# Reordering the head and one change-over of a fused attention, dense-MLP and expert-MLP kernel

## The chip, the cores and the metric

The kernel runs on one core of a Trainium2 chip. The metric is the device time of one execution in microseconds; several executions are given by their median. The engines are PE (TensorE), DVE (VectorE), ACT (ScalarE), POOL (GpSimd) and SP, whose queue issues most DMAs. Each engine runs its own instructions in the order in which the program lists them, and waits on semaphores for the others.

## What is computed

```python
# attention: batch 4, 8 heads, 576 positions, head size 64
scores = q @ k.T / sqrt(64)
cum    = cumsum(max(s, 0))
scores = where(causal, -1e9, scores + minimum(-(cum_i - cum_j), 0))
attn   = softmax(scores)
x      = attn @ v                     # 2304 tokens x 512
# dense MLP, inner size 2048
x      = elu(x @ w_in) @ w_out
# eight experts, inner size 1024, the best one for each token
logits = x @ w_gate + modality_bias[modality_id]
out    = gate * (relu(x @ w1[e]) @ w2[e])
```

Products are made from fp32r operands split into a high and a low part (`qh`, `ql`, `kh`, `kl`, `gh`, `gl`), three matmuls for one product.

## The kernel before

`attention` (L43) works through 16 pairs of heads. For one pair, q and k are loaded as 96 partitions of six positions (`loads`, L103), turned by PE into PSUM and split by ACT (`qh`, `kh`) and DVE (`ql`, `kl`) (`qk`, L162); five blocks of scores S0 to S4 are made (`score`, L197); DVE adds the masked bias and takes row maxima (L236), ACT exponentiates (L243), PE turns the probabilities back (P0 to P4, L279 and L295), and V0 and V1 multiply them with v (`av`, L302). The masks of one pair (`b`, and the diagonal block inside `bias`) are written by POOL from the pair's bias (L136). PSUM has three buffers of two banks for all of this (`ps_t`) and two single banks (`l1_r`, called `l` in the trace).

The order of PE's work in one pair is a list of names written by hand: `ORDER0` for the first pair, `ORDER1` for the second, `ORDER` for the others, `LAST` at the end. "lq" in a list issues loads: q and k of the pair two ahead, then v of this one; "ld" issues the biases of the pair two ahead. SP's queue issues DMAs in that order, and a DMA that waits for a semaphore holds up those behind it.

**The head** (L58 to L68 and L434 to L463). s is loaded on 32 partitions, one for each batch and head; `sums_s` makes the running sums on DVE and stores them to DRAM (`cumd`). From there every later pair's bias is loaded broadcast to 128 partitions (`biases`, L121). The first pair doesn't take that way: `spread` (L443) multiplies, for each of its two heads, a 32-row selector `sel` with the 32 rows of sums, and ACT copies the result to `bias`, in two pieces of 256 and 320 columns. `warm(n)` issues n small matmuls that nothing reads. PE's order in the head is: 40 warm matmuls, q turned, 4 warm, the first spread, k turned, the second spread, 5 warm, the scores S0, S1, S2.

**The change-over** (L1267 to L1277). The dense MLP works on five chunks of tokens in steps f; a step is a first product (`l1`, 12 matmuls of 512 columns, L663 to L665, then ACT and DVE make `gh` and `gl`), and a second product (`l2`, 12 matmuls into four `acc` banks, L998 to L1000). A queue keeps second products two steps behind. The first two first products (`first_step`, L695, "F0" and "F1" in `LAST`) run inside the attention's end, just ahead of V0 and V1 of the last pair. After the attention the loop over `steps` begins with (0, 2); as two steps wait in the queue it first does the second product of step 0, and then the first product of step 2. The `acc` and `tr` rings take the six banks that the attention's `ps_t` has left, `tr` first.

Of the kernel before, what the change touches and what calls it, by code (L numbers as in the profile page):

```python
# [7 lines left out]
F32 = mybir.dt.float32  # L8
# [34 lines left out]
def attention(tc, cst, q, k, v, s, xT, rsd, score_r, extra, first):  # L43
    nc = tc.nc
    B, H, S, D = q.shape
    NP = B * H // 2
    R = B * H
    with ExitStack() as ctx:
# [6 lines left out]
        ident = cst["ident"]  # L55
# [1 line left out]

        cumd = dr.tile([R, S], F32, name="cumd")  # L58
        scr = p1.tile([128, 2, 5, S], F32, tag="pt", name="scr")
        cum, s8, z = (scr[0:R, 0, i] for i in range(3))  # L60
        nc.sync.dma_start(s8, s.rearrange("b h s -> (b h) s"))
        nc.vector.memset(z, 0.0)

        def sums_s():
            nc.vector.tensor_scalar(out=s8, in0=s8, scalar1=0.0, scalar2=8.0, op0=ALU.max, op1=ALU.mult)
            nc.vector.tensor_tensor_scan(out=cum, data0=s8, data1=z, initial=0.0, op0=ALU.add, op1=ALU.add)
            nc.vector.tensor_scalar(out=s8, in0=cum, scalar1=cum[:, S // 2:S // 2 + 1], scalar2=None, op0=ALU.subtract)
            nc.sync.dma_start(cumd, s8)  # L68

        one = st.tile([128, 1], F32, name="one")  # L70
        nc.vector.memset(one, 1.0)
# [31 lines left out]
        def loads(p):  # L103
            b, hp = divmod(p, H // 2)
            d = T[p] = {}

            def qks(which="qk"):
                for n in which:
                    x = {"q": q, "k": k}[n]
                    d[n + "n"] = t = p2.tile([TP, TB, 2, D], F32, tag=n + "n", name=n + "n")  # L110
                    for h in range(2):
                        (nc.scalar if p == 0 and h else nc.sync).dma_start(t[:, :, h], x[b, 2 * hp + h].rearrange("(p t) d -> p t d", t=TB))

            def vs():
                d["vn"] = vn = p2.tile([128, 5, 2, D], F32, tag="vn", name="vn")
                m, r = rows(v, b, hp)
                for h in range(2):
                    nc.sync.dma_start(vn[:, 0:4, h], m[:, :, h])
                nc.sync.dma_start(vn[0:64, 4], r)

            def biases():  # L121
                d["bias"] = bias = p2.tile([128, 2, S], F32, tag="bias", name="bias")
                r0 = b * H + 2 * hp
                nc.sync.dma_start(bias.rearrange("p h s -> p (h s)"),
                                  cumd[r0:r0 + 2].rearrange("h s -> (h s)").unsqueeze(0).to_broadcast([128, 2 * S]))
            d["vs"] = vs
            return qks, biases
# [219 lines left out]
        def unit(p, o):  # L347

            if o[0] == "F":
                return first(int(o[1]))  # L350
            if o[0] == "X":
                x = extra.get((p, int(o[1])))
                return (0, [], x) if x else None
            if o[-1] == "'":
                p, o = p - 1, o[:-1]
            if o[0] == "S":
                return score(p, int(o[1])) if p < NP else None
            if o in OUT:
                return OUT[o](p - 1) if 1 <= p <= NP else None
            if o in ("lq", "ld"):  # L360
                if o == "ld":
                    return 0, extra.get((p, "ld"), []) + ([later.pop(p)] if p in later else []), []
                fs = []
                if p + 2 < NP:
                    qks, later[p] = loads(p + 2)
                    fs = [qks]
                return 0, fs + [T[p]["vs"]], []
            return PREP[o](p + 1) if p + 1 < NP else None
# [62 lines left out]
            for ch in chains:  # L431
                add(now[0] + HOP, d, ch)

        l0, l1 = loads(0), loads(1)  # L434

        sel = scr[0:R, 1, 0, 0:256].rearrange("p (h n) -> p h n", h=2)
        for h in range(2):
            nc.vector.tensor_copy(sel[:, h], ident[0:R, h:h + 1].to_broadcast([R, 128]))
        for f in (l0[0], lambda: l1[0]("k"), sums_s, lambda: l1[0]("q"), l1[1]):
            f()  # L440
        bias = T[0]["bias"] = p2.tile([128, 2, S], F32, tag="bias", name="bias")

        def spread(u, n):  # L443

            def pe():
                x["t"] = t = ps_t.tile([128, 2, 512], F32, tag="t", name="tb")
                for j in range(2):
                    nc.tensor.matmul(t[:, j, 0:n], sel[:, j], s8[:, u:u + n], start=True, stop=True)

            def out():  # L450
                nc.scalar.activation(out=bias[:, :, u:u + n], in_=x["t"][:, :, 0:n], func=AF.Copy)
            x = {}
            return (n / 300, 0, 0), [pe], [[("a", 0.11 + n / 560, out)]]

        warm(WARM)
        u = PREP["q"](0)
        q5 = [u[2][0].pop()]
        for i, x in enumerate((u, spread(0, 256), PREP["k"](0), spread(256, S - 256))):
            issue(x, T[0])
            if i == 0:  # L460
                warm(FILL1)
        run(now[0] + 2.5)
        warm(FILL0)  # L463
        m0 = masks(0)
# [54 lines left out]
def moe(tc, ctx, c, xT, rsd, wi, wo, mid, wg, mb, w1, w2, out, n_pre=3, dbg={}):  # L519
# [144 lines left out]
            nc.tensor.matmul(h, a, xl[:, k], start=False, stop=False)  # L664
            nc.tensor.matmul(h, b, xh[:, k], start=False, stop=(k == KD - 1))  # L665

    def l1(i, f, cu=((), (), ()), tail=()):
        n = chunks[i][1]
        xh, xl = X[i]
        w = W[f]  # L670
        h = l1_r(n)
        l1_mm(h, w, xh, xl)

        for u in tail:
            u()
        for u in cu[0]:
            u()
        er, ghr, glr = (e_r, gh_r, gl_r) if n > 256 else (e_h, gh_h, gl_h)
        e = er(n)
        nc.scalar.activation(out=e, in_=h, func=AF.Relu, scale=-1.0)  # L680
        nc.scalar.activation(out=e, in_=e, func=AF.Exp, scale=-1.0)  # L681
        for u in cu[1]:
            u()
        nc.vector.scalar_tensor_tensor(out=e, in0=e, scalar=-1.0, in1=h, op0=ALU.add, op1=ALU.max)  # L684
        for u in cu[2]:
            u()
        gh = ghr(n)
        gl = glr(n)
        nc.scalar.activation(out=gh, in_=e, func=AF.Copy)  # L689
        nc.vector.tensor_tensor(out=gl, in0=e, in1=gh.bitcast(F32), op=ALU.subtract)  # L690
        G[i, f] = gh, gl
# [47 lines left out]
    rpi_r = Ring(m, 2, 4, I32, "rpi")  # L739
    sr = {}  # L740
    ix_r = Ring(m, 3, 4, I32, "ix")
    tr_r, acc_r = (Ring(ps, n, 512, F32, k) for n, k in ((2, "tr"), (4, "acc")))

    x2d = dbg.get("x2d") or dr.tile([NT + 1, DM], F32, name="x2d")
    wgd = dr.tile([E, DM], F32, name="wgd")
# [519 lines left out]

    ctx.enter_context(tc.manual_schedule(engines=None))
    for i, f in steps:  # L1267
        while len(queue) >= (3 if i == NC - 1 and f > 1 else 2):
            second_product()
        for u in plan.pop((i, f - 0.5), []):  # L1270
            u()
        tail = []
        if i + 1 < NC and f == NF - 1:
            tail = [u[z][2] for u in xu for z in (2, 3)]
        if i == 0 and n_ma <= f + 3 < NF:
            conv_load(f + 3)
        l1(i, f, conv_units(f) if i == 0 else ((), (), ()), tail)  # L1277
        queue.append((i, f))
        if i + 1 < NC:
            if f == NF - 4:  # L1280
                xu = load_x(i + 1)
                for u in xu:
                    u[0][2]()
            if f == NF - 2:
                for u in xu:
                    u[1][2]()
        for u in plan.pop((i, f), []):
            u()
# [163 lines left out]
```

## Time and profile before

| | us |
|---|---|
| runs | 817.70, 817.62, 816.43 |
| median | 817.62 |
| the profiled execution | 818.49 |
| its span, first to last instruction | 816.7 |

| engine | busy us | share of the span |
|---|---|---|
| PE (matmul) | 802.4 | 98% |
| DVE | 560.8 | 69% |
| ACT | 448.6 | 55% |
| POOL | 164.0 | 20% |

Start times in the rows are microseconds from the start of the span. A row's second number is how long one instruction, or the run of `xN` equal ones, was busy; square brackets give the idle time of the engine just ahead of it and what ended it. In the chain of work that ended last, PE has 93% of the span. The mean granted TensorE clock is 0.995 of full speed.

### The profile page before, as it was taken

The numbers are of one execution on the slowest core, as the hardware profiler recorded it, in microseconds if no ns is written. First come the engines' busy times: TensorE is split into PE (matmuls) and PEld (weight loads), VectorE is DVE, ScalarE is ACT, GpSimd is POOL, SyncE is SP. The second block draws the span as 40 slices with busy tenths as digits, with TensorE's granted clock in tenths as the row PEclk, the third lists the DMA queues.
The fourth block names the chain that finished last, engine by engine and source line by source line (L and its number), as shares of the span: only waits on it lengthen the run. The fifth ranks groups of instructions, "written<-read, shape, count | busy, mean of one in ns | idle before, by whom it ended". The sixth has DMA issues, their size and how long they took to land.

```text
span 816.7 us, 14160 instructions
## 1 busy us (share of the span) xinstructions
PE 802.4 (98%) x5037; PEld 682.2 (84%) x5037; DVE 560.8 (69%) x1291; ACT 448.6 (55%) x917; POOL 164.0 (20%) x264
## 2 busy tenths in 40 slices
PE   8999999999999999999999999999999999999995
PEld 7787877877888888888888888899999999999995
DVE  7888888876998587356755575475777656565652
ACT  5898888863776433343334333445655555555542
POOL 5665645530000000200001000203012222212110
PEclk9999999999999999999999999999999999999998
DMA  8998998445644510022000200014737776666651
GB/s 195 241 219 214 222 221 185 137 145 178 201 155 129 190 51 1 1 93 63 1 1 12 92 1 1 1 53 150 222 120 261 256 255 219 231 217 214 222 183 39
DMA packets 123074, 114.14 MB, mean 140 GB/s; under 512 B 67752, under 2 KB 97704, under 8 KB 122866
## 3 DMA queue, kind: packets, MB, share of 16 engines
q1 hardware_dynamic: 118114, 102.87, 43.3%
q0 software_dynamic: 3696, 9.98, 3.4%
q8 instruction: 42, 0.69, 0.4%
q10 hardware_dynamic: 1184, 0.30, 0.2%
q14 instruction: 38, 0.31, 0.1%
HBM read 98.63 MB, written 14.75 MB: 139 GB/s over the span
## 4 chain that ended last, share of the span: by engine, by line
PE 93%; ACT 2%; DVE 2%; DMA 1%; issue 1%; POOL 1%; SPq 0%; POOLq 0%; ACTq 0%
PE acc L998 8%; PE acc L999 8%; PE acc L1000 8%; PE l L665 8%; PE l L664 8%; PE l L663 8%; PE av L315 5%; PE l L1070 4%; PE l L1069 4%; PE l L1068 4%; PE tp L279 4%; PE acc L1089 4%; PE acc L1090 4%; PE acc L1091 4%; PE l L220 3%; PE sc L229 1%
## 5 line engine op out<-in xcount | busy, mean ns | idle before, releaser
L680 ACT ACTIVATE e<-l 128x512 f32<-128x512 f32 (+1 forms) x78 | 43.1, 553 | 147.6 <-PE l L665 138.0
L684 DVE SCALAR_TENSOR_TENSOR e<-e,l 128x512 f32<-128x512 f32 (+1 forms) x78 | 49.3, 632 | 78.1 <-ACT e L681 76.6
L882 POOL DMA_INDIRECT lst<-tk,rpi x18 | 18.4, 1021 | 381.2 <-DVE tk L878 193.4
L243 ACT ACTIVATE pr<-pr,mx 128x128 f32<-128x128 f32 (+4 forms) x144 | 82.5, 575 | 4.9 <-DVE mx L236 3.3
L663 PE MATMUL l<-xsa,wb 128*128 128x512 f32 (+1 forms) x220 | 80.9, 368 | 0.0
L664 PE MATMUL l<-xsa,wb 128*128 128x512 f32 (+1 forms) x220 | 80.9, 368 | 0.0
L665 PE MATMUL l<-xsa,wb 128*128 128x512 f32 (+1 forms) x220 | 80.9, 368 | 0.0
L690 DVE TENSOR_TENSOR gl<-e,gh 128x512 fp32r<-128x512 f32 (+1 forms) x78 | 49.7, 637 | 43.5 <-PE acc L1000 23.0
L998 PE MATMUL acc<-wb,gh 128*128 128x512 f32 x198 | 77.6, 392 | 0.0
L999 PE MATMUL acc<-wb,gh 128*128 128x512 f32 x198 | 77.2, 390 | 0.0
L1000 PE MATMUL acc<-wb,gl 128*128 128x512 f32 x198 | 77.0, 389 | 0.0
L1074 DVE SCALAR_TENSOR_TENSOR gl<-l,gh 128x512 fp32r<-128x512 f32 x36 | 24.9, 690 | 72.3 <-ACT gh L1073 72.3
L689 ACT ACTIVATE gh<-e 128x512 fp32r<-128x512 f32 (+1 forms) x78 | 45.8, 587 | 51.8 <-DVE e L684 51.8
L1073 ACT ACTIVATE gh<-l 128x512 fp32r<-128x512 f32 x36 | 21.5, 597 | 92.7 <-PE l L1070 92.7
L1057 DVE TENSOR_TENSOR wb<-rawa,wb 128x512 fp32r<-128x512 f32 x110 | 68.7, 684 | 3.2 <-ACT e L1321 2.8
L136 POOL TENSOR_SCALAR_AFFINE_SELECT b<-bias 64x576 f32<-64x576 f32 (+3 forms) x80 | 50.6, 651 | 59.9 <-DVE mx L236 52.3
L1056 ACT ACTIVATE wb<-rawa 128x512 fp32r<-128x512 f32 x110 | 60.6, 627 | 0.0
L315 PE MATMUL av<-pt,vn 128*64 128x288 f32 (+4 forms) x512 | 50.2, 342 | 0.0
L1070 PE MATMUL l<-xsa,wb 128*128 128x256 f32 x168 | 47.5, 283 | 0.0
L1069 PE MATMUL l<-xsa,wb 128*128 128x256 f32 x168 | 47.5, 283 | 0.0
L664 PEld LDWEIGHTS l<-xsa,wb 128*128 128x128 f32 x220 | 41.4, 188 | 7.3
L663 PEld LDWEIGHTS l<-xsa,wb 128*128 128x128 f32 x220 | 41.4, 188 | 7.3
(265 smaller groups left out, 2210.5 us busy)
## 6 DMA issues: line engine op xcount, KB each, us to landing
rawa<-in_moe_w_dram SPq DMA_DIRECT2D x80, 512.0 KB
bias<-cumd SPq DMA_DIRECT2D x15, 576.0 KB
rawa<-in_moe_w_in_dram SPq DMA_DIRECT2D x10, 512.0 KB
rawa<-in_moe_w_out_dram SPq DMA_DIRECT2D x10, 512.0 KB
xT<-xo SPq DMA_DIRECT2D x16, 288.0 KB
qn<-in_q_dram SPq DMA_DIRECT2D x31, 144.0 KB
kn<-in_k_dram SPq DMA_DIRECT2D x31, 144.0 KB
vn<-in_v_dram SPq DMA_DIRECT2D x32, 128.0 KB
```

Source lines behind the costliest of these rows:

```text
L243: nc.scalar.activation(out=e[:, 0:w], in_=e[:, 0:w], func=AF.Exp, scale=-1.0, bias=d["mx"][:, i:i + 1], accum_out=sums[p % 2][:, i:i + 1])
L315: nc.tensor.matmul(o[64 * h:64 * h + 64, z, a - 288 * z:e - 288 * z], vn[0:r, j, h], pt[0:r, h, j, a:e], start=(j == 0), stop=(j == js - 1))
L663: nc.tensor.matmul(h, a, xh[:, k], start=(k == 0), stop=False)
L664: nc.tensor.matmul(h, a, xl[:, k], start=False, stop=False)
L665: nc.tensor.matmul(h, b, xh[:, k], start=False, stop=(k == KD - 1))
L998: nc.tensor.matmul(o, gh[:, s], a, start=(f == 0), stop=False)
L999: nc.tensor.matmul(o, gh[:, s], b, start=False, stop=False)
L1000: nc.tensor.matmul(o, gl[:, s], a, start=False, stop=last)
L1056: nc.scalar.activation(out=w[:, x], in_=raw[:, x], func=AF.Copy)
L1057: nc.vector.tensor_tensor(out=w[:, y], in0=raw[:, x], in1=w[:, x].bitcast(F32), op=ALU.subtract)
L1069: nc.tensor.matmul(h[:, j], a, xs[1][:, k], start=False, stop=False)
L1070: nc.tensor.matmul(h[:, j], b, xs[0][:, k], start=False, stop=(k == KD - 1))
```

## The change

Five edits:

1. s is loaded twice, on partitions 0 to 31 and 32 to 63, and its running sums are made on 64 partitions. `sel` has head 0's selector on the first 32 and head 1's on the second, so the two matmuls of a spread read different rows of the array.
2. In the head, the first pair's k is turned directly behind q, and both spreads come after it.
3. The third pair's k is issued on SP's queue ahead of the second pair's biases (`l2[0]("k")`, then `l1[1]()`); in the first pair's "lq" only the third pair's q is left.
4. At the change-over the first product of step 2 comes ahead of the second product of step 0, which is then called from inside `l1` (`mid`), ahead of the writing of `gh`.
5. The `acc` ring takes its banks ahead of `tr`.

```diff
-        cum, s8, z = (scr[0:R, 0, i] for i in range(3))
-        nc.sync.dma_start(s8, s.rearrange("b h s -> (b h) s"))
+        cum, s8, z = (scr[0:2 * R, 0, i] for i in range(3))
+        nc.sync.dma_start(s8, s.rearrange("b h s -> (b h) s").unsqueeze(0).to_broadcast([2, R, S]))
...
-            nc.sync.dma_start(cumd, s8)
+            nc.sync.dma_start(cumd, s8[0:R])
...
-                    qks, later[p] = loads(p + 2)
+                    qks, later[p] = loads(p + 2) if p else (lambda: l2[0]("q"), l2[1])
...
-        l0, l1 = loads(0), loads(1)
-
-        sel = scr[0:R, 1, 0, 0:256].rearrange("p (h n) -> p h n", h=2)
+        l0, l1, l2 = (loads(p) for p in range(3))
+
+        sel = scr[0:2 * R, 1, 0, 0:128]
         for h in range(2):
-            nc.vector.tensor_copy(sel[:, h], ident[0:R, h:h + 1].to_broadcast([R, 128]))
-        for f in (l0[0], lambda: l1[0]("k"), sums_s, lambda: l1[0]("q"), l1[1]):
+            r = slice(R * h, R * h + R)
+            nc.vector.tensor_copy(sel[r], ident[r, R * h + h:R * h + h + 1].to_broadcast([R, 128]))
+        for f in (l0[0], lambda: l1[0]("k"), sums_s, lambda: l1[0]("q")):
             f()
...
-                    nc.tensor.matmul(t[:, j, 0:n], sel[:, j], s8[:, u:u + n], start=True, stop=True)
+                    nc.tensor.matmul(t[:, j, 0:n], sel[R * j:R * j + R], s8[R * j:R * j + R, u:u + n], start=True, stop=True)
...
-            return (n / 300, 0, 0), [pe], [[("a", 0.11 + n / 560, out)]]
+            return (n / 600, 0, 0), [pe], [[("a", 0.11 + n / 560, out)]]
...
-        for i, x in enumerate((u, spread(0, 256), PREP["k"](0), spread(256, S - 256))):
+        for i, x in enumerate((u, PREP["k"](0), spread(0, 256), spread(256, S - 256))):
             issue(x, T[0])
             if i == 0:
                 warm(FILL1)
+            if i == 1:
+                l2[0]("k")
+                l1[1]()
...
-    def l1(i, f, cu=((), (), ()), tail=()):
+    def l1(i, f, cu=((), (), ()), tail=(), mid=None):
...
         for u in cu[2]:
             u()
+        if mid:
+            mid()
         gh = ghr(n)
...
-    tr_r, acc_r = (Ring(ps, n, 512, F32, k) for n, k in ((2, "tr"), (4, "acc")))
+    acc_r, tr_r = (Ring(ps, n, 512, F32, k) for n, k in ((4, "acc"), (2, "tr")))
...
-        while len(queue) >= (3 if i == NC - 1 and f > 1 else 2):
+        begun = (i, f) != steps[0]
+        while begun and len(queue) >= (3 if i == NC - 1 and f > 1 else 2):
             second_product()
...
-        l1(i, f, conv_units(f) if i == 0 else ((), (), ()), tail)
+        l1(i, f, conv_units(f) if i == 0 else ((), (), ()), tail, None if begun else second_product)
```

How instructions stand on the engines, at the three places that the prediction speaks of. First ACT in the head, before; `qh` and `kh` are the split of the first pair's q and k, `bias<-tb` the copies of the two spreads, and the rows of L243 are the first exponentials:

```order
L180 ACTIVATE qh<-tq 128x576
L451 ACTIVATE bias<-tb 128x2x256
L180 ACTIVATE kh<-tk 128x576
L451 ACTIVATE bias<-tb 128x2x320
L243 ACTIVATE pr,sums_134<-pr,mx 128x128 x2
```

and in the changed kernel:

```order
L180 ACTIVATE qh<-tq 128x576
L180 ACTIVATE kh<-tk 128x576
L452 ACTIVATE bias<-tb 128x2x256
L452 ACTIVATE bias<-tb 128x2x320
L243 ACTIVATE pr,sums_134<-pr,mx 128x128 x2
```

`kh` has moved past the first copy of a spread. PE's order has moved in the same way: six turns of k, then the two spreads.

Second SP's queue in the head, before (`L112` are loads of q and k, the first `qn` x2 being the second pair's, `L124` is the second pair's bias, `L118` and `L119` the first pair's v):

```order
L68 DMA cumd<-scr 32x576
L112 DMA qn<-in_q_dram 96x6x64 x2
L124 DMA bias<-cumd 128x1152
L112 DMA qn<-in_q_dram 96x6x64 x2
L112 DMA kn<-in_k_dram 96x6x64 x2
L118 DMA vn<-in_v_dram 128x4x64 x2
L119 DMA vn<-in_v_dram 64x2x64
```

and in the changed kernel:

```order
L68 DMA cumd<-scr 32x576
L112 DMA qn<-in_q_dram 96x6x64 x2
L112 DMA kn<-in_k_dram 96x6x64 x2
L124 DMA bias<-cumd 128x1152
L112 DMA qn<-in_q_dram 96x6x64 x2
L118 DMA vn<-in_v_dram 128x4x64 x2
L119 DMA vn<-in_v_dram 64x2x64
```

The third pair's k has moved past the second pair's bias and past the third pair's q.

Third PE at the change-over, before; `av` is the last pair's output, `gh_99` and `gl_101` are the operands of step 0's second product, `wa_88` the weights of step 2:

```order
L319 MATMUL av<-ident,rs 9x128
L998 MATMUL acc_3264<-wa_86,gh_99 128x512
L999 MATMUL acc_3264<-wa_86,gh_99 128x512
L1000 MATMUL acc_3264<-wa_86,gl_101 128x512
...
L663 MATMUL l_104<-xsa_95,wa_88 128x512
L664 MATMUL l_104<-xsa_96,wa_88 128x512
L665 MATMUL l_104<-xsa_95,wa_88 128x512
```

and in the changed kernel:

```order
L319 MATMUL av<-ident,rs 9x128
L667 MATMUL l_104<-xsa_95,wa_88 128x512
L668 MATMUL l_104<-xsa_96,wa_88 128x512
L669 MATMUL l_104<-xsa_95,wa_88 128x512
...
L1004 MATMUL acc_3262<-wa_86,gh_99 128x512
L1005 MATMUL acc_3262<-wa_86,gh_99 128x512
L1006 MATMUL acc_3262<-wa_86,gl_101 128x512
```

Twelve matmuls into `l_104` have moved past twelve matmuls into the `acc` banks. Behind these 24 the order on PE is as before.

## Rows read from the trace of the kernel before

**Rows 1.** Waits of PE, 0 to 30 us: who for whom, total us, times, longest
```profile
PE tk L173 <- DMA kn<-in_k_dram: 1.6, 1, 1.6
PE tp L279 <- DVE rt L94: 0.2, 1, 0.2
```
**Rows 2.** Waits of PE, 190 us to the end
```profile
PE acc L1342 <- DVE gl L1331: 0.2, 1, 0.2
```
**Rows 3.** Windows at the change-over: length, busy PE, PEld, DVE, ACT, POOL, PEclk, DMA, GB/s
```profile
184.50:186.10 1.60, 0.00 (x0) 0.00 (x0) 0.91 (x4) 1.17 (x2) 0.00 (x0) 1.00 0.00 0
187.00:188.00 1.00, 1.00 (x4) 0.81 (x3) 0.96 (x2) 0.00 (x0) 0.00 (x0) 0.50 0.36 137
```
**Rows 4.** Timeline of PE and its weight loads at the change-over
```profile
184.15 0.28 PE L319 MATMUL av<-ident,rs 128*9 128x128 f32 x1
186.13 0.19 PEld L998 LDWEIGHTS acc<-wa,gh 128*128 128x128 f32 x1 [1.90 <-DVE rt L94]
190.58 0.40 PE L663 MATMUL l<-xsa,wa 128*128 128x512 f32 x1
```
**Rows 5.** Timeline of DVE at the change-over
```profile
181.29 0.68 DVE L713 SCALAR_TENSOR_TENSOR e<-e,l 128x512 f32<-128x512 f32 x1
185.81 0.27 DVE L94 COPY rt<-av 9x128 f32<-9x128 f32 x1
```
**Rows 6.** Timeline of ACT behind the change-over, first instruction of steps 2 and 3
```profile
193.54 0.60 ACT L680 ACTIVATE e<-l 128x512 f32<-128x512 f32 x1 [7.83 <-PE l L665]
198.98 0.60 ACT L680 ACTIVATE e<-l 128x512 f32<-128x512 f32 x1 [2.63 <-PE l L665]
```
**Rows 7.** Timeline of PE in the head
```profile
6.32 1.13 PE L448 MATMUL tb<-scr 32*128 32x256 f32 x4
7.37 0.71 PE L173 MATMUL tk<-ident,kn 96*128 96x96 f32 x6
...
9.89 0.28 PE L220 MATMUL sc<-kl,qh 64*128 64x256 f32 x2
...
10.37 0.28 PE L220 MATMUL sc<-kh,ql 64*128 64x256 f32 x2
...
16.94 0.69 PE L173 MATMUL tk<-ident,kn 96*128 96x96 f32 x6 [1.59 <-DMA kn<-in_k_dram]
17.46 1.04 PE L279 MATMUL tp<-ident,pr 128*128 128x128 f32 x8
```
**Rows 8.** Timeline of ACT in the head
```profile
7.48 0.60 ACT L451 ACTIVATE bias<-tb 128x512 f32<-128x512 f32 x1 [0.63 <-PE tb L448]
8.12 0.65 ACT L180 ACTIVATE kh<-tk 128x576 fp32r<-128x576 f32 x1
...
16.12 0.71 ACT L243 ACTIVATE pr<-pr,mx 128x512 f32<-128x512 f32 x1
```
**Rows 9.** Timeline of POOL in the head
```profile
8.15 0.98 POOL L136 TENSOR_SCALAR_AFFINE_SELECT b<-bias 128x256 f32<-128x256 f32 x2 [5.49 <-ACT bias L451]
...
10.33 2.19 POOL L136 TENSOR_SCALAR_AFFINE_SELECT b<-bias 64x576 f32<-64x576 f32 x3
```
**Rows 10.** Timeline of DVE in the head
```profile
10.82 0.29 DVE L236 CUSTOM_DVE_ANT_0 pr<-sc,b 128x128 f32<-128x128 f32 x1 [1.25 <-PE sc L220]
...
11.93 0.55 DVE L236 CUSTOM_DVE_ANT_0 pr<-l,b 128x384 f32<-128x384 f32 x1
...
18.41 0.76 DVE L184 TENSOR_TENSOR kl<-tk,kh 128x576 fp32r<-128x576 f32 x1
...
20.07 0.69 DVE L236 CUSTOM_DVE_ANT_0 pr<-l,bias 128x512 f32<-128x512 f32 x1
```
**Rows 11.** Windows in the head, columns as in rows 3
```profile
14.00:16.00 2.00, 1.35 (x12) 1.03 (x12) 2.00 (x7) 2.00 (x7) 1.94 (x3) 1.00 0.65 98
16.00:18.00 2.00, 1.06 (x11) 1.09 (x12) 2.00 (x4) 1.19 (x5) 0.73 (x3) 1.00 0.72 171
```
**Rows 12.** SP's queue in the head, the third pair's k
```profile
9.47 1.40 SPq L112 DMA_DIRECT2D kn<-in_k_dram  x2
```

## The prediction

> **What bounds the kernel now.** I read the page first: PE is busy for 98% of the span and has 93% of the chain that ended last. So an edit pays only where PE stands still or runs below full speed. The view of PE's waits says where that is. From 190 us to the end it names one wait, of 0.2 us [rows 2]: whatever PE gains before 190 us reaches the end undiminished. In the first 30 us it names the wait for the third pair's k, 1.6 us, and one of 0.2 us [rows 1].
>
> The change-over is the other place. PE's weight loader stands still for 1.90 us until DVE has copied `rt` out of the last `av` bank, because the first `acc` bank lies there [rows 4, 5]. The windows show what follows: the granted clock is 1.00 while PE stands still, and 0.50, the 1.2 GHz level, from 187 to 188 us [rows 3]. Twelve matmuls then take from 186.13 to 190.58 us, 4.45 us [rows 4]. A step of 24 matmuls at full clock takes 5.44 us, from 193.54 to 198.98 [rows 6], so twelve are worth 2.72.
>
> In the head, PE's own time is not the measure. From 16 to 18 us PE is busy for 1.06 us of 2, while DVE is busy for all of it, and DVE is full from 14 to 16 us too [rows 11]. PE waits there, but DVE is the engine that cannot go faster.
>
> **The change, part by part.**
>
> *The change-over.* The first product of step 2 needs a free `l_104`, which DVE's read of step 0 gives back at 181.29 + 0.68 = 181.97 us [rows 5]. Its weights and tokens were split during the attention. So it can follow L319, at 184.15 us, directly, and the 1.90 us are gone. It takes 2.72 us and ends near 187.0; the `rt` copy ends at 185.81 + 0.27 = 186.08 [rows 5], so the second product of step 0 finds its banks free and PE stands still nowhere. With no standstill I expect no fall of the clock: 4.45 - 2.72 = 1.73 us more. Together 1.90 + 1.73 = 3.63 us, say **3.6**. What the move delays: `gh` of step 2 now waits for the end of step 0's second product, near 189.7 us. It is wanted only by the second product of step 2, which comes 24 matmuls, 5.44 us, after that, and needs the ACT and the DVE pass of about 0.65 us each. That cover holds. The swap of the rings costs nothing, since its first user arrives 0.9 us after the `rt` copy.
>
> *k ahead of the spreads.* k's six turns take the place of the first spread at 6.32 us and end at 6.32 + 0.71 = 7.03 [rows 7]. Before, `kh` started 0.04 us after the turns ended (8.12 against 7.37 + 0.71) [rows 7, 8]; now it starts at 7.08 and ends at 7.73, 1.04 us sooner. So the scores S0 and S1, which end at 10.37 + 0.28 = 10.65 and for which DVE waits until 10.82 [rows 7, 10], end some 0.9 us sooner. But the first copy of a spread now stands behind `kh` on ACT.
>
> *Two spreads at once.* No row shows two 32-row matmuls side by side. The nearest are the scores, pairs of 64-row matmuls of 256 columns: from 9.89 to 10.37 us are four pairs, 0.12 us a pair [rows 7], while one matmul of 512 columns takes 5.44 / 24 = 0.227, so one of 256 about 0.11. A pair costs what one costs. I take the same for 32 rows: the first spread shrinks from 1.13 to about 0.57 us and ends at 7.60. At the other end it stays 1.13 and ends at 8.16.
>
> *What POOL makes of it.* The copy starts when `kh` is done, 7.75, takes 0.60 and ends at 8.35. POOL's first mask came 0.07 us after the copy's end (8.15 against 7.48 + 0.60) [rows 8, 9]; now it comes at 8.42, 0.27 later than before. Without overlap of the two matmuls it is 8.16 + 0.04 + 0.60 + 0.07 = 8.87, 0.72 later. POOL then has no pause until the three masks that start at 10.33 and take 2.19 us; the second of them, the one for S2, ends near 11.8, and DVE takes S2's maximum at 11.93 [rows 9, 10]. POOL was 0.1 us from being late. So the 0.9 us won at S0 and S1 are lost again at S2: DVE takes the early maxima, waits for POOL, and takes S2's near 12.1, 0.2 later than before.
>
> The first spread shows ACT waiting 0.63 us for PE ahead of the copy, and the copy 0.60 us long [rows 8]. The Trainium skill, "TensorEngine Tiling (Array Packing)", section PSUM Bottleneck, says that using parts of the array side by side speeds up the matmuls and not the copying out of PSUM, which can then be the limit. By that rule the overlap is worth little here, since `kh` and the copy set POOL's start; by the rows it still keeps 8.87 - 8.42 = 0.45 us from being lost. No run here shows it yet, and the sum below would be the same under both, as the copy is counted in full.
>
> *k of the third pair earlier.* PE waits 1.59 us for it, until 16.94, though SP issued it at 9.47 [rows 7, 12]: about 7.4 us from issue to use. It now goes out behind the second pair's q, once k of the first pair is turned, near 7.1 us, 2.4 us sooner; so it lands by about 14.5 and PE's wait of 1.59 us goes. What is late next: the turn of the last exponentials, which on ACT end at 16.12 + 0.71 = 16.83 [rows 8], so P3 can start there and not at 17.46 [rows 7]; and DVE, which is full until `kl` of the third pair at 18.41 [rows 10, 11]. `kl` hung on the late k, but by little: DVE, full until 18.00, was idle for at most 0.4 us ahead of it, of which I take half. The next maxima, at 20.07, wait for the scores behind P3, and DVE could have taken them about 0.1 us sooner. So the 1.6 us shrink to 0.3.
>
> *The same k, other side.* The second pair's bias now goes out behind k, near 8.5 us. It feeds POOL's masks of the second pair, whose last, the sixth, is wanted at 20.07 [rows 10]. At 2.19 / 3 = 0.73 us a mask [rows 9], six take 4.4 us: the bias may land as late as 15.7. With the 7.4 us of the slowest load that the rows show, it lands at 15.9. That is a cost of 0.2 at most, and I count none.
>
> *The doubled s* is one more 72 KB load, and the sums on 64 partitions are as long as on 32 (their length is the row's). They were done before 6.32 us, when the first spread read them [rows 7], and are wanted at 7.03 now. Nothing.
>
> *The head in sum.* 0.2 late at S2, of which DVE's next wait, for ACT's `kh` of the second pair, gives 0.1 back; 0.3 gained at k of the third pair: **0.2 gained**. Bounds: 0.9 gained, if POOL isn't late and all of S0's lead gets through; 0.5 lost, if the two matmuls don't overlap (0.72 at POOL, less 0.2).
>
> **The sum.** 3.6 + 0.2 = 3.8 us off. The profiled execution took 818.49 us, its span 816.7; that gives 814.7 for the like of it. It lies 0.87 above the median of the runs, 817.62, so against the median: **813.8 us**.
>
> **The rivals.**
>
> *The clock falls all the same.* The fall at 187 us could hang on something else than the standstill, as PE stood still for 1.59 us at 15 to 17 us and the clock stayed at 1.00 there [rows 7, 11]. Then only the 1.90 us go, and 1.73 stay: 1.9 + 0.2 = 2.1 off, 815.5 us. For it: that second standstill, nearly as long, without a fall. Against it: the only fall of the middle comes directly behind the longest standstill.
>
> *The head's lead gets through.* If POOL starts as early as before, S2 and all behind it move with S0: 0.9 instead of 0.2, 813.1 us. For it: PE, ACT and DVE all have the lead. Against it: POOL's 0.1 us of slack.
>
> *The change doesn't do what it says.* The first product of step 2 waits for something that the order of PE doesn't show, or the second product meets a wait as long behind it. Then the 3.6 us stay and only the head's 0.2 are left: 817.4 us. Against it: DVE is done with `l_104` 2.2 us before PE needs it.
>
> *Slower than before.* One mechanism: the second pair's bias, behind k in SP's queue. Each microsecond by which it lands after 15.7 us puts off the second pair's maxima, and PE behind them. It eats up 3.6 us where it lands after 19.3 us; at 21 us the kernel ends at 817.6 - 3.6 + 5.3 = 819.3 us. For it: loads of the head are slow, 7.4 us for k. Against it: it would need 10.8 us, half as long again as the slowest one seen.
>
> **How the numbers follow.** 0.2% is 1.6 us, about what a measurement of this kernel can tell from no change. Forecast 0.70, head's lead 0.12, clock 0.10, no effect at the change-over 0.05, late bias 0.03. The first three are faster by more than 1.6 us: 0.92. No effect is within 0.2%: 0.05. Slower: 0.03. The range takes in the head's lead at the low end (813.1, less 0.6 as the runs lie apart by 1.27) and the clock at the high end (815.5 and 0.2): 812.5 to 815.7.
>
> **What would show it.** At the change-over: the first product of step 2 directly behind L319 of the last pair, no wait named for `rt`, PEclk 1.00 from 184 to 191 us, and step 3's first ACT row 3.6 + 0.2 sooner than 198.98, near 195.2. In the head: `kh` near 7.1 us, the first mask near 8.4, S2's maximum at 12.0 to 12.2 with an idle time ended by POOL, no wait for the third pair's k, and the maximum of 20.07 near 19.8. The prediction is wrong if the clock falls at another place, if a load of weights that PE now reaches 3.8 us sooner isn't there, or if S2's maximum comes before 11.5 us.

## The result, and the profile after

The changed kernel takes **821.70 us** (median of 6 runs, 821.23 to 822.02) and the kernel before 817.02 us (median of 6) beside it. The ratio is **1.0055, with a 95% interval of 1.0042 to 1.0068**: slower by 4.7 us, where 813.8 us and a gain of 3.8 were forecast; it is outside the range of 812.5 to 815.7 too. The runs of the kernel before lie further apart than the 1.27 us of the table, 815.7 to 820.0 us over all that follows, so the comparisons below are ratios with intervals.

Span of the profiled execution: 820.2 us, against 816.7. Its waits of PE in the first 30 us, and those of DVE (who for whom, total us, times, longest), answer to [rows 1]:

```profile
PE tq L173 <- DMA qn<-in_q_dram: 4.5, 1, 4.5
PE tp L279 <- DVE pt L94: 1.3, 1, 1.3
...
DVE scr L65 <- DMA scr<-in_s_dram: 6.2, 1, 6.2
```

The wait for the third pair's k is gone, as forecast. A wait for the *first* pair's q stands in its place, which no line of the prediction speaks of, and the sums wait 6.2 us for s. The windows of the changed kernel (length, busy time of PE, PEld, DVE, ACT, POOL, granted clock, DMA share, GB/s) show what the transfers do meanwhile:

```profile
4.00:6.00 2.00, 1.57 (x15) 1.30 (x13) 0.00 (x0) 0.00 (x0) 0.00 (x0) 1.00 1.34 178
6.00:8.00 2.00, 0.00 (x0) 0.00 (x0) 0.00 (x0) 0.00 (x0) 0.00 (x0) 1.00 1.17 133
8.00:10.00 2.00, 0.00 (x0) 0.00 (x0) 1.10 (x2) 0.00 (x0) 0.00 (x0) 1.00 0.17 30
```

From 4 to 6 us, with the loads under way, the view gives a DMA share of 1.34. From 8 us it is 0.17, and 30 GB/s move, until 11 us: by 0.17 / 1.34 x 16 that is, as an estimate, the work of two engines of 16. DVE has the doubled s, issued first, at 8.87 us, where it was 2.73 before. The 312 packets from 8.5 to 11 us are all under 512 bytes, where a row of s has 2304: what still comes then was issued behind s, as q was, for which PE waits until 10.05 us. PE's turns of q before, and the start of its work in the changed kernel, with DVE's maximum behind it, from the timelines (start, duration, engine, line, operation, tiles; idle time ahead in brackets), answer to [rows 7, 10]:

```profile
5.36 0.80 PE L173 MATMUL tq<-ident,qn 96*128 96x96 f32 x6
```
```profile
10.05 1.20 PE L173 MATMUL tq<-ident,qn 96*128 96x96 f32 x6 [4.48 <-DMA qn<-in_q_dram]
...
11.46 1.17 PE L173 MATMUL tk<-ident,kn 96*128 96x96 f32 x6
12.56 2.29 PE L449 MATMUL tb<-scr 32*128 32x256 f32 x8
...
16.02 0.41 PE L220 MATMUL sc<-kh,ql 64*128 64x256 f32 x2
16.24 0.41 PE L220 MATMUL sc<-kh,qh 64*128 64x256 f32 x2
16.45 0.41 PE L220 MATMUL sc<-kl,qh 64*128 64x256 f32 x2
...
27.14 0.69 DVE L236 CUSTOM_DVE_ANT_0 pr<-l,bias 128x512 f32<-128x512 f32 x1
```

q's turns start at 10.05 us. k's six turns take 1.17 us and not 0.71, and the pairs of the scores follow each other by 0.21 us and not by 0.12 [rows 7]: TensorE runs at nearly half its pace, until 20.0 us. (The clock's column reads 1.00 there, but this trace has no clock record before 20.07 us; the last section shows what that means.) Both together are the loss: the maximum that stood at 20.07 [rows 10] stands at 27.14 us, 7.07 later, and the last pair's L319 starts 7.17 later than at 184.15 [rows 4].

The change-over did what was forecast. PE's timeline there, ACT's first instructions of steps 1 and 3, and two windows, for [rows 3, 4, 6]:

```profile
191.32 0.28 PE L319 MATMUL av<-ident,rs 128*9 128x128 f32 x1
191.36 0.47 PE L667 MATMUL l<-xsa,wa 128*128 128x512 f32 x1
...
189.69 0.58 ACT L713 ACTIVATE e<-l 128x512 f32<-128x512 f32 x1
...
202.54 0.60 ACT L684 ACTIVATE e<-l 128x512 f32<-128x512 f32 x1 [5.03 <-PE l L669]
...
191.00:193.00 2.00, 2.00 (x14) 1.62 (x13) 1.30 (x3) 1.17 (x2) 0.00 (x0) 1.00 0.00 0
193.00:195.00 2.00, 2.00 (x10) 1.65 (x10) 1.97 (x4) 0.60 (x1) 0.00 (x0) 1.00 0.43 160
```

The first product of step 2 (L667) follows L319 directly, the granted clock stays at 1.00, and PE names no wait for `rt`. From ACT's first instruction of step 1 to that of step 3 are 12.85 us. Before it was 16.44, from 182.54 to 198.98 [rows 6]:

```profile
182.54 0.58 ACT L707 ACTIVATE e<-l 128x512 f32<-128x512 f32 x1
```

So the change-over gives 3.59 us, the head takes 7.15 (189.69 against 182.54), and 3.56 of loss are left, which is the spans' difference of 3.5.

### The profile page after: what moved, and what is told of

It is laid out like the page before. It is cut to its first block, busy times and chain, and to the rows that moved or that the text cites. A ratio compares the mean times of both kernels' runs of the same rounds, so it can differ in the third digit from the quotient of the medians.

```text
span 820.2 us, 14161 instructions
## 1 busy us (share of the span) xinstructions
PE 803.4 (98%) x5037; PEld 683.7 (83%) x5037; DVE 561.2 (68%) x1291; ACT 449.4 (55%) x917; POOL 165.5 (20%) x264
## 4 chain that ended last, share of the span: by engine, by line
PE 95%; ACT 1%; DVE 1%; DMA 1%; issue 0%; POOL 0%; SPq 0%; POOLq 0%; DVEq 0%
PE acc L1004 8%; PE l L669 8%; PE l L668 8%; PE l L667 8%; PE acc L1005 8%; PE acc L1006 8%; PE av L315 5%; PE l L1076 4%; PE l L1075 4%; PE l L1074 4%; PE tp L279 4%; PE acc L1095 4%; PE acc L1096 4%; PE acc L1097 4%; PE l L220 3%; PE sc L229 1%
## 5 line engine op out<-in xcount | busy, mean ns | idle before, releaser
L243 ACT ACTIVATE pr<-pr,mx 128x128 f32<-128x128 f32 (+4 forms) x144 | 82.5, 575 | 5.8 <-DVE mx L236 4.3
L667 PE MATMUL l<-xsa,wb 128*128 128x512 f32 (+1 forms) x220 | 80.9, 368 | 0.0
L1076 PE MATMUL l<-xsa,wb 128*128 128x256 f32 x168 | 47.5, 283 | 0.0
L1075 PE MATMUL l<-xsa,wb 128*128 128x256 f32 x168 | 47.5, 283 | 0.0
L1074 PE MATMUL l<-xsa,wb 128*128 128x256 f32 x168 | 47.5, 283 | 0.0
L668 PEld LDWEIGHTS l<-xsa,wb 128*128 128x128 f32 x220 | 41.4, 188 | 7.3
```

The lines of the kernel that those rows point to most:

```text
L243: nc.scalar.activation(out=e[:, 0:w], in_=e[:, 0:w], func=AF.Exp, scale=-1.0, bias=d["mx"][:, i:i + 1], accum_out=sums[p % 2][:, i:i + 1])
L667: nc.tensor.matmul(h, a, xh[:, k], start=(k == 0), stop=False)
L1074: nc.tensor.matmul(h[:, j], a, xs[0][:, k], start=(k == 0), stop=False)
L1075: nc.tensor.matmul(h[:, j], a, xs[1][:, k], start=False, stop=False)
L1076: nc.tensor.matmul(h[:, j], b, xs[0][:, k], start=False, stop=(k == KD - 1))
```

## The experiments

Twelve kernels were timed, in 5 to 12 executions each. "q" is the start of q's turns, "last pair" the start of `kl` of the last pair (what the head is late by is read there), "steps 1 to 3" the change-over's stretch as above; these three are from each kernel's profiled execution, in us.

| kernel | us | before | ratio, 95% interval | q | last pair | steps 1 to 3 |
|---|---|---|---|---|---|---|
| before | | | | 5.36 | 153.91 | 16.44 |
| the change | 821.70 | 817.02 | 1.0055 (1.0042 to 1.0068) | 10.05 | 161.05 | 12.85 |
| e1 two loads | 814.97 | 817.92 | 0.9966 (0.9954 to 0.9979) | 6.18 | 156.51 | 12.87 |
| e2 doubled s alone | 825.32 | 817.92 | 1.0088 (1.0073 to 1.0102) | 9.74 | 163.34 | 16.43 |
| e2b copies inner | 818.13 | 818.02 | 1.0009 (0.9993 to 1.0024) | 6.44 | 154.93 | 16.43 |
| e3 change-over alone | 815.56 | 817.92 | 0.9968 (0.9956 to 0.9980) | 5.36 | 155.32 | 12.83 |
| e4 head, two loads | 818.20 | 817.92 | 0.9994 (0.9983 to 1.0005) | 6.40 | 156.32 | 14.81 |
| e5 q first | 816.91 | 818.02 | 0.9982 (0.9970 to 0.9994) | 4.79 | 156.94 | 12.89 |
| e6 more fillers | 814.82 | 818.02 | 0.9959 (0.9945 to 0.9972) | 6.49 | 155.36 | 12.88 |
| e7 q first, old head | 820.59 | 818.02 | 1.0032 (1.0019 to 1.0045) | 5.04 | 159.89 | 12.85 |
| e9 second subtraction | 814.20 | 817.86 | 0.9961 (0.9947 to 0.9974) | 5.73 | 156.30 | 12.89 |
| e10 with 45 fillers | 814.32 | 817.86 | 0.9959 (0.9944 to 0.9973) | 5.46 | 154.85 | 12.88 |
| e11 bias ahead of k | 814.08 | 817.86 | 0.9957 (0.9943 to 0.9971) | 5.36 | 154.32 | 12.88 |
| e12 spread first | 813.04 | 817.84 | 0.9944 (0.9926 to 0.9962) | 5.33 | 153.02 | 12.89 |

### Is it the load of s? (e1, e2, e2b)

**e1**, the change with s loaded by two DMAs:

```diff
-        nc.sync.dma_start(s8, s.rearrange("b h s -> (b h) s").unsqueeze(0).to_broadcast([2, R, S]))
+        for j in range(2):
+            nc.sync.dma_start(s8[R * j:R * j + R], s.rearrange("b h s -> (b h) s"))
```

> All edits of the change stay; the doubled s is loaded by two loads of 32 rows each instead of one load with a leading dimension of two copies. Theory A (the one load with two copies is served by only a few of the 16 DMA engines, and q, which lies behind it on these, comes 4.5 us late): q's turns start at 5.4 to 5.9 us without a wait for its load, DMA moves over 150 GB/s from 3 us until all is there, and the time is 813 to 815 us. Theory B (the order is to blame: k's turns ahead of the spreads, the third pair's k and the bias behind it): q or the sums stay late and the time stays within 1 us of 821.7. Theory C (the doubled bytes are to blame, 144 KB instead of 72): a delay of under 0.5 us, 814 to 815 us, with q late by 0.3 to 0.5 us.

**e2**, the kernel before with that one load and nothing else:

```diff
-        cum, s8, z = (scr[0:R, 0, i] for i in range(3))
-        nc.sync.dma_start(s8, s.rearrange("b h s -> (b h) s"))
+        cum, s8, z = (scr[0:2 * R, 0, i] for i in range(3))
+        nc.sync.dma_start(s8, s.rearrange("b h s -> (b h) s").unsqueeze(0).to_broadcast([2, R, S]))
...
-                    nc.tensor.matmul(t[:, j, 0:n], sel[:, j], s8[:, u:u + n], start=True, stop=True)
+                    nc.tensor.matmul(t[:, j, 0:n], sel[:, j], s8[0:R, u:u + n], start=True, stop=True)
```

> The kernel before with the doubled s load alone (one load with two copies into 64 rows; the spreads read the first 32 as before). Theory A: q's turns wait about 4.5 us, the sums about 6 us, and the time is 823 to 825 us (817 and the 7.2 us by which the head of the changed kernel is late). Theory B: no change, 816.5 to 817.5 us. Theory C: 817 to 817.6 us.

**e2b**, the same bytes into as many rows, with the copies as the inner dimension:

```diff
-        nc.sync.dma_start(s8, s.rearrange("b h s -> (b h) s"))
+        nc.sync.dma_start(s8, s.rearrange("b h s -> (b h) s").unsqueeze(1).to_broadcast([R, 2, S]))
...
```

(The lines left out give every second row weight 0 in the selector and skip it in the store of the sums.)

> The kernel before with s loaded once into 64 rows, 144 KB as in the change, but with the two copies as the inner and the 32 rows as the outer dimension; the spreads read 64 rows of which every second is a copy with weight 0. Theory A (the leading dimension of two confines the load to a few engines): no wait of 4 us for q, q at 5.4 to 6.3 us, DMA at 150 GB/s and more until all is there, 817 to 819.5 us. Theory C (a source that repeats is slow in itself, or the bytes are): q's turns wait 4 us as with the doubled s alone, about 825 us.

The load alone makes the kernel before 7.4 us slower (825.32 against 817.92). With two loads, all five edits together are 2.95 us faster than before. (e2's profiled execution, with the last pair 9.43 us late, is the longest of its six, 827.62.) With the copies inside, 144 KB from a repeating source leave the median where it was; they are not free, as PE waits 1.49 us for q and the last pair comes 1.02 us late. Waits of PE in the first 12 us of e2, then of e1, and the window from 9 to 10 us of e2 and from 6 to 8 us of e2b:

```profile
PE tq L173 <- DMA qn<-in_q_dram: 4.2, 1, 4.2
```
```profile
PE tq L174 <- DMA qn<-in_q_dram: 0.6, 1, 0.6
```
```profile
9.00:10.00 1.00, 0.26 (x2) 0.29 (x3) 0.97 (x2) 0.00 (x0) 0.00 (x0) 0.53 0.17 31
```
```profile
6.00:8.00 2.00, 1.56 (x13) 1.43 (x14) 0.67 (x3) 0.65 (x1) 0.00 (x0) 1.00 0.99 154
```

That is theory A, and the doubled bytes (C) and the order (B) are out as the main cause. The leading dimension of two decides. The Trainium skill, "DMA: Bandwidth & Descriptors", section "Rules for kernel authors", says it in one line: "an outermost dim of size c < 16 — e.g. a leading zero-stride broadcast of c copies — confines the whole DMA to at most c engines". These traces agree: with the two copies outermost, a share worth two engines by the estimate above from 8 to 11 us in the changed kernel and from 9 to 11 us in e2, and no such stretch with 32 rows outermost (0.99 from 6 to 8 us in e2b, 0.77 from 8 to 11).

C is not nothing, though: q is still 0.8 us late with two loads (6.18 against 5.36) and 1.1 with e2b.

### The two halves of the change (e3, e4)

**e3** is the kernel before with edits 4 and 5 of the change's list, **e4** is e1 without them.

> The kernel before with the two edits at the change-over alone (first product of step 2 ahead of the second product of step 0, rings in the other order). If the change-over gives what the prediction said (1.90 us of standstill and 1.73 us of a fallen clock): 813.2 to 813.6 us, granted clock 1.00 from 184 to 191 us, step 3's first ACT row near 195.4. If the gain seen in the changed kernel hangs on its late head: 815 us or more.

> The head's edits without those at the change-over, s by two loads of 32 rows. Theory A and the prediction's sum for the head: 0.2 us faster than before, 816.1 to 817.5 us (bounds of the prediction: 0.9 faster to 0.5 slower); the third pair's k isn't waited for, and the first maximum of S2 comes at 12.0 to 12.2 us. Theory B: about 7 us slower than before, 823 to 825 us.

In both traces, and in that of every kernel with these edits, steps 1 to 3 take 12.83 to 12.89 us: 3.6 us less than 16.44, whatever the head did. The granted clock is 1.00 through it. But e3's time fell by 2.4 us only, a miss. Its trace shows one cause in the head, where e3 has no edit. PE's timeline and the window behind it:

```profile
5.36 1.17 PE L173 MATMUL tq<-ident,qn 96*128 96x96 f32 x6
...
10.00:13.00 3.00, 3.00 (x24) 2.41 (x22) 1.02 (x8) 1.22 (x4) 2.77 (x6) 0.51 0.99 253
```

The six turns of q took 1.17 us and not 0.80, the clock read 0.51, about the 1.2 GHz level, from 10 to 13.5 us, and the head was 1.41 us late (155.32 against 153.91). The other cause is in what is compared. In e4 PE stands still for `rt` as before, 1.67 us, and yet the clock did not fall behind it:

```profile
187.69 0.50 PE L1003 MATMUL acc<-wa,gh 128*128 128x512 f32 x1 [1.67 <-DVE rt L95]
```
```profile
188.00:190.00 2.00, 2.00 (x10) 1.64 (x9) 1.97 (x2) 0.00 (x0) 0.00 (x0) 1.00 0.40 156
```

Steps 1 to 3 take 14.81 us there. So 1.63 of the 3.6 us (16.44 - 14.81) are only to be won in executions in which the clock falls. It fell in three of the four traces without the edits.

The timed executions say more, as each has its mean granted clock on record. The 77 of the kernel before that stand beside the experiments lie in three groups: 20 at 0.996 to 0.998, which took 815.7 to 817.1 us; 37 at 0.994 to 0.996 and 817.5 to 818.5 us, as the profiled one with its one fall; 20 at 0.992 or 0.993 and 819.0 to 820.0 us. By an estimate, that one fall, 3.4 us at 0.50, lowers the mean by 3.4 x 0.50 / 817 = 0.002. e3's ten executions lie in two groups: four at 0.996 or 0.997 and 814.0 to 814.6 us, six at 0.994 or 0.995 and 815.5 to 816.3. The medians of the two best groups are 1.7 us apart (816.20 and 814.47), about the standstill alone; e3's best group is 3.4 us under the middle one of before, whose median is 817.9. So what the edits give depends on the falls that an execution has, and e3's median lies in its second group, as does its profiled execution with the fall in the head. Where the falls lie in executions that were not profiled is not shown.

e4's time is that of before, above the 816.1 to 817.5 expected: with two loads and q late by 1.04 us, the head's edits win nothing. (In its trace the clock is at 0.50 from 8.8 to 15.6 us, and the last pair comes 2.41 us late.)

### Bringing q sooner (e5, e6, e7)

**e5** is e1 with both loads of s behind q's load on SP; **e7** is e3 with its one load of s behind q's; **e6** is e1 with `WARM` at 48 instead of 40.

```diff
...
-        for f in (l0[0], lambda: l1[0]("k"), sums_s, lambda: l1[0]("q")):
+        for f in (lambda: l0[0]("q"), load_s, lambda: l0[0]("k"), lambda: l1[0]("k"), sums_s, lambda: l1[0]("q")):
```

> All edits, s by two loads of 32 rows, and these issued behind q's first load on SP instead of ahead of it. Theory A (PE stands still for 0.6 us because q is issued 0.45 us later, and this standstill is what makes TensorE run at half pace from 6.2 to 13.5 us, as S0's pairs, 0.21 us apart instead of 0.12, show): q's turns start at 5.3 to 5.5 us without a wait, S0's pairs are 0.12 us apart, and the time is 1.5 to 2.2 us under that of two loads ahead of q, 812.6 to 813.5 us where before is 817.9; its span is near the predicted 812.9. Theory B (the head's edits themselves leave gaps in which TensorE loses its pace, whenever q comes): S0's pairs stay 0.21 us apart and the time stays within 0.5 us of 815.0. Theory C (s is now late): the sums end after 7.5 us, the first spread waits for them, and half the gain is lost, 814 us.

> The kernel before with the change-over's edits and with s, one load of 32 rows, behind q's first load. Theory A: PE has q when its filler matmuls end, no loss of pace in the head, third pair's k waited for as before: 3.6 us under a run of before whose head also kept its pace, 812.6 to 813.4 us; against the same with all of the head's edits it shows what these are worth where the pace holds (by the prediction 0.2 us, bounds 0.9 gained to 0.5 lost). Theory B: the same as the change-over's edits alone, 815.3 to 815.8 us.

> As with two loads ahead of q, and the filler matmuls ahead of q's turns are 48 instead of 40, so that PE works on until q is there near 6.2 us. Theory A (the standstill costs the pace): q's turns start at 6.3 to 6.6 us, S0's pairs are 0.12 us apart, and the time falls by 1.2 to 2 us from 815.0, to 813.0 to 813.8 us. Theory B (the lateness of q costs, not the standstill): 0.1 to 0.4 us more than 815.0, S0's pairs 0.21 us apart.

e5 and e7 are misses. In e5 theory C's mechanism holds, at more than its price (816.91, where 814 was expected), and e7 shows the same. Waits of PE in e5, then in e7:

```profile
PE tk L176 <- DMA kn<-in_k_dram: 1.8, 1, 1.8
...
PE tb L452 <- DVE scr L70: 0.5, 1, 0.5
```
```profile
PE tb L450 <- DVE scr L69: 2.4, 1, 2.4
```

s came 2 to 3 us later (the sums start at 6.68 us in e5, 4.71 in e1; at 5.88 in e7, 2.73 in the kernel before). q's turns started 0.3 to 0.6 us sooner than before, but for another reason: they follow the 40 fillers, without a wait, and these took 3.83 and 4.08 us instead of 4.45. That q itself landed sooner than before is not shown. From 2 to 6 us the loads fill the DMA queues (200 and 217 GB/s and a share up to 1.31 in the kernel before), and what is put behind comes later: here s has to stay first, and be small.

e6 is a miss in time (0.15 us under e1, where 1.2 to 2 were expected), though its own trace does what theory A says: S0's pairs 0.12 us apart and the last pair 1.15 us sooner than in e1's. In e1's profiled execution TensorE had half pace up to 13.5 us; its times (814.1 to 817.4 us, the profiled one 816.35) say that most of its executions may have had less of that. e6's lie within 814.2 to 815.4.

### The doubling made on the chip, and the order (e9 to e12)

**e9**: all edits, one load of s as before, and the second copy of the sums from a second subtraction on DVE; **e10** has 45 fillers besides:

```diff
...
+            nc.vector.tensor_scalar(out=s8d[R:2 * R], in0=cum, scalar1=cum[:, S // 2:S // 2 + 1], scalar2=None, op0=ALU.subtract)
...
```

> All edits of the change, but s is loaded once, into 32 rows as before, and the second copy of the sums is made on DVE, by a second subtraction of 0.51 us into rows 32 to 63 (DVE is idle there, from 5.1 to 6.9 us). Theory A (the head's loss is the load of s alone: few engines in the change, and with two loads q and the sums 1 to 2 us late): q's turns start at 5.3 to 5.6 us as before, the sums end by 5.7, S0's first maximum comes at 9.8 to 10.0 us (0.9 sooner than before), the span is 812 to 813.3 us and the time 3.4 to 5 us under before. Theory B (the head's order costs by itself, the second pair's bias behind k above all): POOL waits over 2 us for that bias, the head ends later than before and the time is within 0.5 us of the change-over's edits alone (2.4 under before) or worse.

> The same with 45 filler matmuls instead of 40 ahead of q's turns, 0.5 us more. If TensorE's pace in the head hangs on whether PE stands still for q, some executions with 40 lose it and none with 45: the median is 0 to 1 us lower and the runs lie closer together. If the pace is safe with 40: 0.3 to 0.5 us more.

e9 is 3.7 us faster than before, 0.9961: theory A, and the change without its load, against a forecast of 3.8 for the whole. POOL waits for no bias (0.4 us in e10, 0.7 in the change). (Its profiled execution, 814.7 us of span, took the longest of its seven: the granted clock was 0.50 from 15 to 22 us, and S0's first maximum came at 10.22, as q's turns were 0.37 late.) e10 has the same median within 0.12 us, and its runs lie closer together (814.0 to 815.1 against 813.9 to 816.4). In its profiled execution the clock fell all the same, from 15.2 to 18.6 us, so the fillers ahead of q are not all that it hangs on.

**e11**: e9 with the second pair's bias ahead of the third pair's k on SP.

> The same as with the second subtraction and 40 fillers, and the second pair's bias goes out ahead of the third pair's k instead of behind it. Theory B (the late bias costs what the early k gains): POOL no longer waits for the bias, 0.3 to 0.6 us faster than with k first. The prediction's view (the bias has 7 us of cover, the early k is worth 0.3): 0.1 to 0.4 us slower than with k first, or the same.

No difference (814.08 against 814.20): the bias behind k isn't the rival that I made of it, nor is its early place worth anything. **e12** is e11 with the first spread ahead of k again:

```diff
-        for i, x in enumerate((u, PREP["k"](0), spread(0, 256), spread(256, S - 256))):
+        for i, x in enumerate((u, spread(0, 256), PREP["k"](0), spread(256, S - 256))):
...
```

> As the kernel with the second subtraction and the bias ahead of the third pair's k, but the first pair's k is turned behind the first spread again, as in the kernel before; both heads are still spread at once. It undoes the change's edit of k ahead of the spreads alone. Theory A (POOL's masks set the first stage: with k first the copy of the first spread waits on ACT behind kh, POOL starts near 8.9 us and DVE waits 1.0 us for it at S2): POOL's first mask comes near 7.7 us, DVE doesn't wait for POOL at S2, and the time is 0.4 to 0.9 us lower, 813.2 to 813.7 where before is 817.9. Theory B (what PE and ACT save by turning k first counts too): S0 comes 0.6 us later, S2's maximum at the same time, no difference over 0.2 us.

POOL and DVE in e11, then in e12 (the first mask; the three masks; S2's first maximum), for [rows 9, 10]:

```profile
8.88 0.98 POOL L138 TENSOR_SCALAR_AFFINE_SELECT b<-bias 128x256 f32<-128x256 f32 x2 [6.22 <-ACT bias L454]
...
11.06 2.19 POOL L138 TENSOR_SCALAR_AFFINE_SELECT b<-bias 64x576 f32<-64x576 f32 x3
...
12.54 0.56 DVE L238 CUSTOM_DVE_ANT_0 pr<-l,b 128x384 f32<-128x384 f32 x1 [1.02 <-POOL b L138]
```
```profile
7.59 0.98 POOL L138 TENSOR_SCALAR_AFFINE_SELECT b<-bias 128x256 f32<-128x256 f32 x2 [4.93 <-ACT bias L454]
...
9.77 2.19 POOL L138 TENSOR_SCALAR_AFFINE_SELECT b<-bias 64x576 f32<-64x576 f32 x3
...
11.25 0.56 DVE L238 CUSTOM_DVE_ANT_0 pr<-l,b 128x384 f32<-128x384 f32 x1
```

POOL starts 1.29 us sooner, DVE no longer waits 1.02 us for it, and the last pair comes 1.30 us sooner, 0.89 ahead of the kernel before. Of these, 0.43 us are the slow turns of q in e11's profiled execution (1.16 us), so about 0.9 us are the order's. At 813.04 us, a little under the 813.2 to 813.7 expected and **0.9944 of before (0.9926 to 0.9962)**, it is the fastest of all: edit 2 of the change, k ahead of the spreads, costs about 1 us. (The intervals of e11 and e12 overlap; the point rests on the two traces. The planner also put S1's maxima ahead of S0's in e12, so not all else is equal.)

## Why the prediction was wrong, and where it was right

**The step that failed** is one sentence: the doubled s "is one more 72 KB load", "wanted at 7.03 now. Nothing." I counted bytes and the time until the sums are wanted, and not how the transfer is spread over the engines, nor what lies behind it on them. It is not one more load but one load in another shape. By e2 it costs 7.4 us, and the head of the changed kernel is 7.15 us late. None of the rivals held it: the one that ended slower was a late load, but the bias, not q.

Of the 7.15 us, q's lateness is 4.69 (10.05 against 5.36); the other 2.46 are put down to the slower pace until 20 us, by difference. That TensorE has its full pace in the head was never a step of the prediction, and should have been one. Before, the pace rose at 5.64 us, just behind the fillers' end; in the changed kernel PE stood still then, and it rose at 20.07.

**The change-over** was right: 3.6 us forecast, 3.59 measured, and 3.55 to 3.61 in all other traces with the edits. The first product follows L319, the clock does not fall, no wait takes the place of the one removed, and the swap of the rings costs nothing. The rival "the clock falls all the same" is out. What was missing is the lesson of e3 and e4: the 1.73 us for the clock were taken from one execution, as if each one lost them.

**The head** was right but for s. e11 has the prediction's head, but for the bias's place and the second subtraction; the turns of q end 0.43 us late in its profiled execution (k's start at 6.75, not 6.32). Take that off, and `kh` is at 7.11 us (7.08 forecast), the first mask at 8.45 (8.42), S0's maximum at 9.90 (10.82 - 0.9 = 9.92), and S2's at 12.11, with a wait for POOL ("near 12.1"). Only the 0.3 us at the third pair's k did not come: PE's wait for it is gone in e1, e9 and e11, but the maximum of 20.07 comes at 20.04 by the same count (20.47 less 0.43). So the head's edits are worth nothing instead of 0.2. The rival "the head's lead gets through" is out: S2's maximum waits for POOL, as forecast.

**Two spreads at once** do run side by side, though the first takes 0.70 us and not the 0.57 forecast. PE's timeline in e12, where the granted clock is 1.00, against 1.13 and 1.34 us one after the other before:

```profile
6.15 0.70 PE L451 MATMUL tb<-scr 32*128 32x256 f32 x4
...
7.52 0.81 PE L451 MATMUL tb<-scr 32*128 32x320 f32 x4
```

That e9 takes off 3.7 us, where 3.8 were forecast for the whole, is partly luck. By the spans of e11 and of the kernel before (812.4 and 816.7), 4.3 us are gone: 3.56 at the change-over, 0.86 between the last pair's `kl` and step 1 (27.77 us instead of 28.63) and 0.3 behind step 3, less 0.41 by which the head is late. The 0.86 is in no term of the sum; the last section tells what is known of it. What made the forecast fail is the one term that was put at nothing without a row.

## What to carry to other kernels

Read a DMA's access pattern by its outermost dimension before its bytes: two copies in front put 144 KB on two engines, by the estimate above, and PE waited 4.5 us for what lay behind it, here the first operand of the whole kernel. A copy that an idle engine can make (0.51 us of DVE) leaves the queues free: with it q's turns start at 5.36 to 5.73 us, with a second load at 6.18, though the times (814.20 and 814.97 us) do not separate the two. And where a chain's order is changed, look for the engine that sets the stage, here POOL, and start *its* feed first; what the others gain ahead of it is lost again.

## What the runs showed of the hardware

- In every trace TensorE begins at half pace: the fillers come 0.107 us apart. In e5 they come 0.056 us apart from 4.2 us on. The clock records of each trace begin where the pace rises, between 4.14 and 6.93 us in twelve of the traces, at 13.53 in e1 and at 20.07 in the changed kernel. Where there is no record yet, the views show 1.00. The windows of the kernel before and of e5 have the same 1.00 beside 12 and 18 matmuls:

```profile
4.00:5.00 1.00, 1.00 (x12) 1.00 (x11) 0.96 (x2) 0.00 (x0) 0.00 (x0) 1.00 1.26 227
```
```profile
4.00:5.00 1.00, 1.00 (x18) 1.00 (x17) 0.00 (x0) 0.00 (x0) 0.00 (x0) 1.00 1.08 197
```

  So pairs of scores 0.21 us apart beside 1.00 (the changed kernel, e1) and beside 0.50 (e4) are the same half pace. The spacing of equal matmuls shows it either way.
- The length of one standstill does not tell whether the granted clock falls. In the head it fell to 0.50 near the end of PE's waits of 4.17 us (e2), 2.38 (e7) and 1.77 (e5), about 2 us behind one of 1.15 (e10), one of 1.07 (e9) and one of 0.87 (e4), and in e3 at 10.0 us with no wait of PE since its fillers began; behind 1.59 (before, at 16.94 us), 1.49 (e2b) and 1.44 (e6, e11) it did not.
- Two of DVE's instructions (the split of a token block) and a long one of POOL that overlap take different times, depending on which starts first. In the kernel before DVE's start 0.18 us ahead of POOL's, in e6 0.14 behind it (DVE, then POOL, of each):

```profile
163.14 2.29 DVE L650 TENSOR_TENSOR xsa<-rawa,xsa 128x512 fp32r<-128x512 f32 x2
...
163.32 3.30 POOL L566 TENSOR_SCALAR xga<-rawa 128x1024 f32<-128x1024 f32 x1
```
```profile
164.54 1.27 DVE L655 TENSOR_TENSOR xsa<-rawa,xsa 128x512 fp32r<-128x512 f32 x2
...
164.40 4.12 POOL L571 TENSOR_SCALAR xga<-rawa 128x1024 f32<-128x1024 f32 x1
```

  DVE's two take 1.02 us less where POOL is ahead, and POOL's takes 0.82 more (spans of POOL are rough). From the last pair's `kl` to step 1 the kernel takes 27.76 us in e6 and 28.63 before. e1 and the change, which have the same order on every engine but for the load of s, differ in the same way (27.78 and 28.64). It came out as in e6 in e4, e5 and e9 to e12 too, and as before in e2, e2b, e3 and e7. What makes the one or the other, and whether the 0.87 us hang on it, wasn't tried.
